# The end of the first MoE in a retention + MoE + MoE kernel: a weight slice split earlier, a rounding on another engine, two blocks and the logits in another order

## The chip, the cores and the metric

The kernel runs on one core of a Trainium2 chip. The core has TensorE (matmuls, results in PSUM banks), VectorE, ScalarE and GpSimd (elementwise work), and SyncE, which issues DMAs. Each engine runs its own queue in order and waits on semaphores for the others. The metric is the device time of one execution in microseconds.

## The reference

Three layers in a row: a retention (attention with a decaying state), a dense feed-forward layer with the mish activation ("the first MoE"), and a mixture of eight experts in which each token goes to the one expert with the largest logit.

```python
x = attn_out.transpose(0, 2, 1, 3).reshape(B * S, H * D)     # 1536 tokens x 512

h = x @ w_in                                                 # 512 x 2048
sp = np.where(h > 20.0, h, np.log1p(np.exp(np.minimum(h, 20.0))))
x = (h * np.tanh(sp)) @ w_out                                # mish, 2048 x 512

logits = x @ w_gate                                          # 8 experts
e_idx = np.argmax(logits, axis=1)
gate_w = softmax(logits)[np.arange(N), e_idx]
eom = 1.0 / (1.0 + np.exp(-(x @ w_output_gate)))
for e in range(E):
    mask = e_idx == e
    h = np.maximum(x[mask] @ w1[e], 0.0)
    out[mask] = gate_w[mask, None] * eom[mask, e, None] * (h @ w2[e])
```

## The kernel before

**Numbers.** Every large product is made of three fast matmuls: each operand is split into a rounded part and a remainder (`hi`, `lo`), and hi·hi, hi·lo and lo·hi are added in PSUM. So a weight slice or an activation must be *rounded* (a cast, `copy`, L311) and then have its *remainder* taken (a subtraction on VectorE) before TensorE can use it. For weights this is `split` (L221): `split_in` for `w_in`, with the rounding on ScalarE, and `split_out` for `w_out`, with both steps on VectorE (`split(..., V, V)`). The split slices of `w_out` live in a ring of six tiles, that is three slices.

**The first MoE.** The 1536 tokens are worked on in two groups of six blocks of 128 tokens. Per group there are 16 slices of 128 hidden units; slice `i` runs from 0 to 31 over both groups. For a slice, `up` multiplies (into `hps`), `take_h` copies the result and takes a sigmoid on ScalarE, `mish_ln` and `mish_tanh` make mish from it: a logarithm and a tanh on ScalarE, each with a table load ahead of it where the table changes, and then a product on VectorE (L263). `mish_split` rounds this product (L267, on the engine given to it) and takes its remainder on VectorE (L268). `down` adds the slice's contribution to the six accumulators `acc[0]` to `acc[5]`, one per block of tokens: three matmuls (L278, L279, L280) for each block. L278 and L279 need the rounded activation, L280 its remainder.

Logarithm and tanh run for two slices at a time, save for the last two, 30 and 31 (`NS - 2`, `NS - 1`), which run one by one. `down` is three slices behind `up`, so after the loop over slices `down` of 29, 30 and 31 remain.

**The stage after the loop** (L725 to L788) joins the first MoE with the routing of the last six blocks. Block by block (`tb`) it ends the accumulation of slices 30 and 31, takes the finished rows out (`take_rows`, and `part_rows` with a rounding on ScalarE, L496, and a subtraction on GpSimd, L497), turns the rows of the block before (`turn_rows`, four TensorE transposes, L318, and a copy), and for pairs of blocks makes the logits (`logits_of`, L339), turns them (`turn_logits`, L349 and the copy L350), picks the expert (`pick`, `weigh`, L363 to L384, small VectorE operations), ranks the tokens (`rank`, two matmuls, L393 and L394), finds their places (`place`, L402 to L406), builds a selection matrix (`select`, L485) and sends the rows to their places in DRAM (`send`, VectorE and indirect DMAs from GpSimd's queue, L421). Instead of reading the rows of expert 0 back from DRAM, TensorE adds them: `turn_base` (L472) starts the banks with what was already there, and `add_rows` (L504) multiplies the selection with the rows. When the last pair is in, `split_x` makes the input of expert 0, and the second MoE begins.

**What sets the order.** TensorE, VectorE and ScalarE run in the order in which the code issues (`manual_schedule`); there is no planner for them. GpSimd's and SyncE's queues are ordered by the scheduler of the framework.

Of the kernel before, what the change touches and what calls it, by code (L numbers as in the profile page):

```python
# [65 lines left out]
def retention_moe_moe(ctx: ExitStack, tc: tile.TileContext, qkv, wraw, w12, wg, cst, pad, out):  # L66
    nc = tc.nc
    V, A, T, G, SP = nc.vector, nc.scalar, nc.tensor, nc.gpsimd, nc.sync
# [15 lines left out]
    def he(w, dtype=F32):  # L84

        return h_p.tile([P, GT], dtype, name="h")[:, 0:w]

    acc, hps = [], []
# [141 lines left out]
    NS = NG * NF  # L230
# [26 lines left out]
    def mish_ln(b):  # L257
        for i in b:
            A.activation(out=es[i], in_=es[i], func=AF.Ln, bias=tiny)

    def mish_tanh(i):
        A.activation(out=es[i], in_=es[i], func=AF.Tanh, scale=-1.0)  # L262
        V.tensor_tensor(out=hs[i], in0=hs[i], in1=es.pop(i), op=ALU.mult)  # L263

    def mish_split(i, engine):
        h, gh, gl = hs.pop(i), he(GT, F32R), he(GT, F32R)
        copy(engine, gh, h)  # L267
        V.tensor_tensor(out=gl, in0=h, in1=gh.bitcast(F32), op=ALU.subtract)  # L268
        gs[i] = gh, gl

    def down(i, tbs):
        g, f = divmod(i, NF)
        wh, wl = wout[i]
        gh, gl = gs[i]
        for tb in tbs:
            o = acc[tb]
            c = slice(tb * P, (tb + 1) * P)
            T.matmul(out=o, lhsT=gh[:, c], rhs=wh, start=(f == 0), stop=False)  # L278
            T.matmul(out=o, lhsT=gh[:, c], rhs=wl, start=False, stop=False)  # L279
            T.matmul(out=o, lhsT=gl[:, c], rhs=wh, start=False, stop=(f == NF - 1))  # L280
        if tbs[-1] == GB - 1:
            del wout[i], gs[i]
# [28 lines left out]
    def copy(engine, to, of):  # L311
        (A.copy if engine is A else engine.tensor_copy)(out=to, in_=of)  # L312

    def turn_rows(b, o, engine):
        r = rows[b // 2][:, b % 2]
        x = he(KD * P)
        for k in range(KD):
            T.transpose(out=o[:, k * P:(k + 1) * P], in_=r[:, k * P:(k + 1) * P], identity=ident)  # L318
        copy(engine, x, o)
        xts[b] = [x[:, k * P:(k + 1) * P] for k in range(KD)]  # L320
# [13 lines left out]
    def logits_of(b0, n, o):  # L334

        w, v = 32 * n, int(b0 < NB - GB)
        for k in range(KD):
            for b in range(n):
                T.matmul(out=o[b * 32:(b + 1) * 32, 0:P], lhsT=wgs[:, v, k], rhs=xts[b0 + b][k],  # L339
                         start=(k == 0), stop=(k == KD - 1))  # L340
        x = [xts.pop(b0 + b) for b in range(n)][0]
        lt, l = spare.pop(b0) if v else x[0:2]
        lt, l = lt[0:w], l[:, 0:w]
        A.copy(out=lt, in_=o[0:w, 0:P])
        return lt, l
# [9 lines left out]
    def tl(name, n, w, dtype=F32):  # L355
        return r_p.tile([P, n, w], dtype, name=f"{name}{n}", bufs=3 if n == 2 else 1)
# [19 lines left out]
    def weigh(b0, n, o):  # L376

        lz = o.rearrange("p (b e) -> p b e", b=n)
        l, z = lz[:, :, 0:E], lz[:, :, E:2 * E]
        m, ohb = chosen[b0]["m"], chosen[b0]["ohb"]  # L380
        d, t = tl("d", n, E + 1), tl("t", n, E)
        V.tensor_tensor(out=d[:, :, 0:E], in0=l, in1=m.to_broadcast([P, n, E]), op=ALU.subtract)
        V.tensor_tensor(out=t, in0=z, in1=ohb, op=ALU.mult)
        V.tensor_reduce(out=d[:, :, E:E + 1], in_=t, axis=AX.X, op=ALU.add, negate=True)  # L384
        chosen[b0]["d"] = d

    def exps(b0):
        d = chosen[b0]["d"]
        A.activation(out=d, in_=d, func=AF.Exp)
# [77 lines left out]
    def turn_base(banks):  # L467

        r = xrow[0]
        for k in banks:  # L470
            for b in range(2):
                T.matmul(out=xbank[k][:, b * CB2:(b + 1) * CB2], lhsT=r[0:CB2, b, k * P:(k + 1) * P],  # L472
                         rhs=ident[0:CB2, 0:CB2],
                         start=(not begun[k]), stop=False)
                begun[k] = True
# [24 lines left out]
    def add_rows(b0, n, banks, last=False):  # L500
        for k in banks:
            for b in range(b0, b0 + n):
                for i, x in enumerate(parts[b]):
                    T.matmul(out=xbank[k][:, 0:CAP], lhsT=x[:, k * P:(k + 1) * P], rhs=sel[b], start=(not begun[k]),  # L504
                             stop=(last and b == b0 + n - 1 and i == 1))
                    begun[k] = True
# [89 lines left out]
    def split_in(i):  # L596
        if i < NS:
            win[i] = split(fw[i % NF][:, 0], "wi")

    def split_out(i):  # L600
        if 0 <= i < NS:
            wout[i] = split(fw[i % NF][:, 1], "wo", V, V)
# [27 lines left out]
    with tc.manual_schedule(engines={A.engine, T.engine, V.engine}):  # L630
# [36 lines left out]
        for i in range(NS):  # L667
            b, c = batch_at.get(i - 1, []), batch_at.get(i - 2, [])
            j = i - NF - LAG
            s0 = ND + 4 * min(i, 3) + 34 * max(0, i - 3) // 5 + 2  # L670
            mish_ln(b)
            steps_to(s0)
            late = range(NA + 2 * i, min(NA + 2 * i + 2, NU))
            if late:
                sm = scores(late[0], acc[0:2])
            up(i, 0)
            if late:
                values(late[0], acc[0:2], sm)
                sm = scores(late[1], acc[2:4])
                for n in late:  # L680
                    if n + 2 < NU:
                        prep_unit(n + 2)
            split_out(i + 2 - LAG)
            take_h(i, 0)
            if len(c) == 2:
                mish_split(c[1], A)
            if b:
                mish_tanh(b[0])
            split_in(i + 2)
            steps_to(s0 + 2)  # L690
            up(i, 1)
            if late:
                values(late[1], acc[2:4], sm)
            take_h(i, 1)
            if len(b) == 2:
                mish_tanh(b[1])
            if b:
                mish_split(b[0], A)

            if j == 1:  # L700
                turn_pair(0)
                turn_pair(2)
            if j == 3:
                turn_pair(4)
            steps_to(s0 + 4)
            if i >= LAG:
                down(i - LAG, range(0, 3))
                route(j)
                down(i - LAG, range(3, GB))
            if j == -1:  # L710
                for tb in range(GB):
                    take_rows(tb, A if tb % 2 else V)
                    if tb % 2:
                        keep(tb - 1)
            if j == 0:
                r = x_p.tile([P, KD * GT], F32, name="xl")
                for tb in range(0, GB, 2):
                    xpair[tb] = load_blocks(xall[tb * P:(tb + 2) * P], r[:, 512 * tb:512 * tb + 1024])
            if j == 10:
                load_rows(0)  # L720
            if 6 <= i < 6 + E:
                A.dma_start(out=xs[(i - 6) * CAP:(i - 5) * CAP], in_=pad)
            if j >= 0:
                load_w12(j)
        g = NG - 1  # L725
        b0 = g * GB
        mish_ln([NS - 1])
        mish_tanh(NS - 1)
        mish_split(NS - 1, A)
        split_out(NS - 1)  # L730
        down(NS - 3, range(GB))
        for m in range(NF - LAG, NF):
            load_w12(m)
        splits2(0, True, True)
# [2 lines left out]
        la, ra, rc, lb, rb = (acc[0][:, 0:4 * E], acc[1][:, 0:2 * E], acc[1][:, 2 * E:4 * E], hps[1][:, 0:4 * E],  # L737
                              acc[1][:, 4 * E:6 * E])
        for tb in range(GB):
            down(NS - 2, [tb])  # L740
            if tb:
                turn_rows(b0 + tb - 1, hps[tb % 2], V if tb < 3 else A)
            if tb in (3, 5):
                n = b0 + tb - 3
                lg[0] = turn_logits(acc[0], *lg[0])
                pick(n, 2, lg[0])
                weigh(n, 2, lg[0])
            if tb == 4:
                turn_base([0, 1])
                add_rows(b0, 2, [0])  # L750
            if tb == 5:
                turn_base([2])
            down(NS - 1, [tb])
            if tb in (3, 5):
                o = ra if tb == 3 else rc
                rank(n, 2, o)
                place(n, 2, o)
                select(n, 0)
                select(n, 1)
            if tb == 4:  # L760
                add_rows(b0, 2, [1])
            take_rows(b0 + tb, A)
            part_rows(b0 + tb, acc[tb])
            if tb in (3, 5):
                exps(n)
                send(n, 2)
            if tb in (2, 4):
                lg[0] = logits_of(b0 + tb - 2, 2, acc[0])
        add_rows(b0, 2, [2])
        turn_rows(b0 + 5, hps[0], A)  # L770
        logits(b0 + 4, lb[:, 0:2 * E])
# [169 lines left out]
```

## Time and profile before

| what | value |
|---|---|
| median of 3 runs | 563.82 us (563.41 to 564.87) |
| the profiled execution | 561.92 us |
| its span, first to last instruction | 560.2 us |
| TensorE matmul busy | 539.9 us (96% of the span) |
| VectorE busy | 369.2 us (66%) |
| ScalarE busy | 378.6 us (68%) |
| GpSimd busy | 75.7 us (14%) |
| mean granted TensorE clock | 0.993 |

All rows below are of the one profiled execution. A timeline lists, for one engine, when an instruction started, how long it took, its line, what it wrote and read with the shape, how often in a row it ran, and in brackets how long the engine had been idle before it and who released it. Matmuls are pipelined, so a matmul of 0.39 us can follow its predecessor after 0.23 us. The granted clock is a share of full speed: 1.00 is 2.4 GHz. Idle time of an engine counts only where the chain of waits runs through it.

### The profile page before, as it was taken

To read this page: it belongs to the slowest core of one execution; us is meant where nothing else is said; L and a number is where in the kernel's file an instruction comes from. 1 tells how busy PE (TensorE), PEld (TensorE's weight loads), DVE (VectorE), ACT (ScalarE), POOL (GpSimd) and SP (SyncE) were. 2 spreads that over 40 slices of the span, in tenths; PEclk is the share of its full clock that TensorE was granted. 3 is DMA by queue.
4 is the path that set the end of the run, shared out by engine and by line. 5 is a ranking of instruction groups with operands and counts; after the bars stand their busy time and mean duration, and the time that the engine had idled before them with its cause. 6 is when DMAs were issued, how large, how long until landed. Compare 5 with 4: busy or idle time off the path is not lost.

```text
span 560.2 us, 9429 instructions
## 1 busy us (share of the span) xinstructions
PE 539.9 (96%) x3311; PEld 451.9 (81%) x3311; DVE 369.2 (66%) x790; ACT 378.6 (68%) x722; POOL 75.7 (14%) x130
## 2 busy tenths in 40 slices
PE   8999989999999999999999997989999999999992
PEld 4555578899899999989898895778888888888881
DVE  3788867888888753655356435587777677677560
ACT  5667649978887886767767777445766666666551
POOL 3445410000000100000001500530101101101001
PEclk9999999999999999999999999999999999999997
DMA  8889721245454102661221621327999866671001
GB/s 304 290 262 297 261 77 65 78 147 167 154 179 138 42 1 76 175 163 45 70 76 37 220 78 45 144 84 190 220 295 340 269 214 206 212 212 52 2 22 36
DMA packets 38116, 83.22 MB, mean 149 GB/s; under 512 B 5858, under 2 KB 15970, under 8 KB 37936
## 3 DMA queue, kind: packets, MB, share of 16 engines
q1 hardware_dynamic: 34848, 71.70, 41.8%
q0 software_dynamic: 2240, 6.31, 3.4%
q10 hardware_dynamic: 976, 4.56, 2.6%
q8 instruction: 28, 0.46, 0.3%
q14 instruction: 24, 0.20, 0.1%
HBM read 73.04 MB, written 13.72 MB: 155 GB/s over the span
## 4 chain that ended last, share of the span: by engine, by line
PE 86%; DVE 4%; issue 4%; ACT 2%; DMA 1%; POOL 0%; POOLq 0%; DVEq 0%; ACTq 0%
PE hps L244 23%; PE hps L534 13%; PE acc L278 7%; PE acc L279 7%; PE acc L280 7%; PE acc L551 5%; PE acc L550 5%; PE acc L552 5%; PE sp L148 4%; PE sp L165 2%; PE sp L169 2%; PE sp L173 1%; DMA cs<-in_cst_dram 1%; DMA h<-in_qkv_dram 1%; PE acc L148 1%
## 5 line engine op out<-in xcount | busy, mean ns | idle before, releaser
L244 PE MATMUL hps<-xh,wi 128*128 128x384 f32 x512 | 137.8, 338 | 0.0
L534 PEld LDWEIGHTS hps<-xh,wi 128*128 128x128 f32 x768 | 95.3, 191 | 7.4 <-DVE h L539 1.0
L534 PE MATMUL hps<-xh,wi 128*128 128x224 f32 x768 | 96.0, 274 | 0.8 <-DVE h L539 0.8
L244 PEld LDWEIGHTS hps<-xh,wi 128*128 128x128 f32 x512 | 93.1, 188 | 1.8 <-ACT h L255 0.3
L244 PE MATMUL hps<-xl,wi 128*128 128x384 f32 x256 | 85.7, 335 | 0.0
L225 DVE TENSOR_TENSOR wi<-fw,wi 128x512 fp32r<-128x512 f32 x96 | 66.2, 689 | 19.7 <-ACT wi L312 12.5
L278 PE MATMUL acc<-wo,h 128*128 128x512 f32 x192 | 75.9, 395 | 2.6 <-DVE wo L312 2.6
L279 PE MATMUL acc<-wo,h 128*128 128x512 f32 x192 | 75.4, 393 | 0.2 <-DVE wo L225 0.2
L280 PE MATMUL acc<-wo,h 128*128 128x512 f32 x192 | 75.5, 393 | 0.0
L225 DVE TENSOR_TENSOR wo<-fw,wo 128x512 fp32r<-128x512 f32 x96 | 66.3, 691 | 12.2 <-ACT wo L312 9.1
L263 DVE TENSOR_TENSOR h<-h 128x768 f32<-128x768 f32 x32 | 30.7, 959 | 50.6 <-ACT h L262 47.0
L254 ACT ACTIVATE h<-hps 128x384 f32<-128x384 f32 x64 | 31.4, 491 | 48.2 <-PE hps L244 48.2
L312 ACT CAST wi<-fw 128x512 fp32r<-128x512 f32 x96 | 59.0, 615 | 0.5 <-DVE fw L218 0.5
L538 ACT ACTIVATE h<-hps 128x224 fp32r<-128x224 f32 x64 | 22.8, 357 | 44.1 <-PE hps L534 43.1
L551 PE MATMUL acc<-wo,h 128*112 128x512 f32 x128 | 50.7, 396 | 0.0
L550 PE MATMUL acc<-wo,h 128*112 128x512 f32 x128 | 50.6, 395 | 0.0
L552 PE MATMUL acc<-wo,h 128*112 128x512 f32 x128 | 50.3, 393 | 0.0
L244 PEld LDWEIGHTS hps<-xl,wi 128*128 128x128 f32 x256 | 48.1, 188 | 1.2
L312 ACT CAST wo<-fw 128x512 fp32r<-128x512 f32 x64 | 39.7, 621 | 11.1 <-PE acc L551 11.0
L142 ACT ACTIVATE qz<-h,cs 128x128 f32<-128x128 f32 x96 | 33.2, 394 | 19.6 <-PE sp L148 16.6
L278 PEld LDWEIGHTS acc<-wo,h 128*128 128x128 f32 x192 | 36.1, 188 | 10.3 <-ACT wo L312 3.0
L280 PEld LDWEIGHTS acc<-wo,h 128*128 128x128 f32 x192 | 36.0, 188 | 7.9 <-DVE h L268 0.3
(140 smaller groups left out, 812.7 us busy)
## 6 DMA issues: line engine op xcount, KB each, us to landing
fw<-in_w_dram SPq DMA_DIRECT2D x64, 512.0 KB, 4.1
raw<-in_wraw_dram SPq DMA_DIRECT2D x32, 512.0 KB, 3.9
h<-in_qkv_dram SPq DMA_DIRECT2D x48, 256.0 KB, 5.2
xs<-in_pad_dram ACTq DMA_DIRECT2D x8, 449.8 KB
raw<-xs SPq DMA_DIRECT2D x28, 112.0 KB, 7.8
xall<-raw SPq DMA_DIRECT2D x6, 512.0 KB, 4.8
xl<-xall SPq DMA_DIRECT2D x12, 128.0 KB, 4.6
raw<-xs SPq DMA_DIRECT2D x2, 224.0 KB, 3.2
```

The source lines that it names most:

```text
L142: A.activation(out=qz[:, j], in_=t[:, 0], func=AF.Copy, scale=halves[:, j:j + 1])
L225: engine.tensor_tensor(out=lo, in0=src, in1=hi.bitcast(F32), op=ALU.subtract)
L244: T.matmul(out=o, lhsT=a[:, k * P:(k + 1) * P], rhs=b[:, k, c], start=(n == 0), stop=(n == 3 * KD - 1))
L254: A.activation(out=hs[i][:, c], in_=o, func=AF.Copy)
L278: T.matmul(out=o, lhsT=gh[:, c], rhs=wh, start=(f == 0), stop=False)
L279: T.matmul(out=o, lhsT=gh[:, c], rhs=wl, start=False, stop=False)
L280: T.matmul(out=o, lhsT=gl[:, c], rhs=wh, start=False, stop=(f == NF - 1))
L312: (A.copy if engine is A else engine.tensor_copy)(out=to, in_=of)
L534: T.matmul(out=o, lhsT=a[:, k * P:(k + 1) * P], rhs=x[:, k, b:b + CAP], start=(n == 0), stop=(n == 3 * KD - 1))
L550: T.matmul(out=o, lhsT=g[:, c], rhs=wh, start=(f == 0), stop=False)
L551: T.matmul(out=o, lhsT=g[:, c], rhs=wl, start=False, stop=False)
L552: T.matmul(out=o, lhsT=g[:, l], rhs=wh, start=False, stop=(f == NF2 - 1))
```

## The change

Four edits, all around the end of the loop over slices:

- In the loop's last iteration, the rounding of slice 30 (`mish_split(b[0], ...)`) goes from ScalarE to VectorE.
- `split_out(31)` is issued ahead of `mish_tanh(31)` and `mish_split(31)`, not behind them.
- `down` of slice 30 runs for blocks 0 and 1 before the loop over blocks. In the loop it runs from block 2 on, and the transposes of block 0's rows come behind slice 31's matmuls of block 1.
- For blocks 3 and 5 the logits are turned, picked and weighed ahead of the transposes of the rows, not behind them. `turn_base([2])` goes from block 5 of the loop to behind the loop.

```diff
--- before.py
+++ after.py
@@ -695,7 +695,7 @@
             if len(b) == 2:
                 mish_tanh(b[1])
             if b:
-                mish_split(b[0], A)
+                mish_split(b[0], A if i < NS - 1 else V)
 
             if j == 1:
                 turn_pair(0)
@@ -725,10 +725,11 @@
         g = NG - 1
         b0 = g * GB
         mish_ln([NS - 1])
+        split_out(NS - 1)
         mish_tanh(NS - 1)
         mish_split(NS - 1, A)
-        split_out(NS - 1)
         down(NS - 3, range(GB))
+        down(NS - 2, [0, 1])
         for m in range(NF - LAG, NF):
             load_w12(m)
         splits2(0, True, True)
@@ -737,20 +738,21 @@
         la, ra, rc, lb, rb = (acc[0][:, 0:4 * E], acc[1][:, 0:2 * E], acc[1][:, 2 * E:4 * E], hps[1][:, 0:4 * E],
                               acc[1][:, 4 * E:6 * E])
         for tb in range(GB):
-            down(NS - 2, [tb])
-            if tb:
-                turn_rows(b0 + tb - 1, hps[tb % 2], V if tb < 3 else A)
+            if tb > 1:
+                down(NS - 2, [tb])
             if tb in (3, 5):
                 n = b0 + tb - 3
                 lg[0] = turn_logits(acc[0], *lg[0])
                 pick(n, 2, lg[0])
                 weigh(n, 2, lg[0])
+            if tb > 1:
+                turn_rows(b0 + tb - 1, hps[tb % 2], V if tb < 3 else A)
             if tb == 4:
                 turn_base([0, 1])
                 add_rows(b0, 2, [0])
-            if tb == 5:
-                turn_base([2])
             down(NS - 1, [tb])
+            if tb == 1:
+                turn_rows(b0, hps[1], V)
             if tb in (3, 5):
                 o = ra if tb == 3 else rc
                 rank(n, 2, o)
@@ -766,6 +768,7 @@
                 send(n, 2)
             if tb in (2, 4):
                 lg[0] = logits_of(b0 + tb - 2, 2, acc[0])
+        turn_base([2])
         add_rows(b0, 2, [2])
         turn_rows(b0 + 5, hps[0], A)
         logits(b0 + 4, lb[:, 0:2 * E])
```

On VectorE, at the end of the loop over slices (L263 is the mish product, L268 the remainder, `L312 CAST h` a rounding of an activation, `L312 CAST wo` and `L225` rounding and remainder of an output slice):

```order
 L263 TENSOR_TENSOR h<-h 128x768
-L268 TENSOR_TENSOR h<-h 128x768
-L263 TENSOR_TENSOR h<-h 128x768
-L268 TENSOR_TENSOR h<-h 128x768
-L312 CAST wo<-fw 128x512
-L225 TENSOR_TENSOR wo<-fw,wo 128x512
+L312 CAST h<-h 128x768
+L268 TENSOR_TENSOR h<-h 128x768
+L312 CAST wo<-fw 128x512
+L225 TENSOR_TENSOR wo<-fw,wo 128x512
+L263 TENSOR_TENSOR h<-h 128x768
+L268 TENSOR_TENSOR h<-h 128x768
```

The rounding of slice 30 is new on this engine, and the two steps of the last output slice now stand ahead of the product of slice 31.

On TensorE, behind the first blocks of `down` (acc_1076 and acc_1077 are the accumulators of blocks 0 and 1):

```order
+L278 MATMUL acc_1077<-wo,h 128x512
+L279 MATMUL acc_1077<-wo,h 128x512
+L280 MATMUL acc_1077<-wo,h 128x512
 L278 MATMUL acc_1076<-wo,h 128x512
 L279 MATMUL acc_1076<-wo,h 128x512
```

Three matmuls of slice 30, for block 1, now stand ahead of the first matmul of slice 31 (the last two rows).

On TensorE, at block 5 of the stage after the loop (L349 turns the logits, L318 the rows, L472 is `turn_base`, L393 and L394 rank):

```order
+L349 MATMUL acc_1076<-cs,h 128x64
 L318 MATMUL hps_1075<-cs,raw 128x128 x4
-L349 MATMUL acc_1076<-cs,h 128x64
-L472 MATMUL acc_1080<-cs,raw 128x112 x2
 L278 MATMUL acc_1081<-wo,h 128x512
 L279 MATMUL acc_1081<-wo,h 128x512
 L280 MATMUL acc_1081<-wo,h 128x512
```

The logits are turned before the rows, and `turn_base` has left its place ahead of slice 31's matmuls; it stands behind L394 in the new order. At block 3 the two turns change places in the same way.

## Rows read from the trace of the kernel before

**Rows 1.** The page, part 4: chain that ended last, shares by engine.

```profile
PE 86%; DVE 4%; issue 4%; ACT 2%; DMA 1%; POOL 0%; POOLq 0%; DVEq 0%; ACTq 0%
```

**Rows 2.** Table by stretches: engine busy us (instructions), granted clock, DMA share, GB/s.

```profile
400.00:450.00 50.00, 50.00 (x334) 43.83 (x333) 36.04 (x65) 32.07 (x66) 6.49 (x6) 1.00 1.01 293
343.00:348.00 5.00, 2.17 (x9) 1.08 (x7) 4.00 (x7) 3.06 (x6) 0.00 (x0) 1.00 0.09 15
550.00:561.00 11.00, 0.08 (x1) 0.00 (x0) 0.00 (x0) 0.69 (x1) 1.56 (x2) 0.62 0.15 45
```

**Rows 3.** Timeline, ScalarE: start, us, line, operation, out<-in, [idle before <-releaser].

```profile
336.35 0.49 ACT L255 ACTIVATE h<-hps 128x384 f32<-128x384 f32 x1
337.23 0.84 ACT L312 CAST h<-h 128x768 fp32r<-128x768 f32 x1 [0.39 <-DVE h L263]
338.09 1.28 ACT L259 ACT_TABLE_LOAD   x1
...
343.51 0.83 ACT L312 CAST h<-h 128x768 fp32r<-128x768 f32 x1 [1.03 <-DVE h L263]
```

**Rows 4.** Timeline, VectorE, the last product and the last split.

```profile
342.52 0.96 DVE L263 TENSOR_TENSOR h<-h 128x768 f32<-128x768 f32 x1 [3.46 <-ACT h L262]
344.37 0.96 DVE L268 TENSOR_TENSOR h<-h 128x768 fp32r<-128x768 f32 x1 [0.90 <-ACT h L312]
345.25 0.42 DVE L312 CAST wo<-fw 128x512 fp32r<-128x512 f32 x1
345.77 0.69 DVE L225 TENSOR_TENSOR wo<-fw,wo 128x512 fp32r<-128x512 f32 x1
```

**Rows 5.** Timeline, TensorE, before and after its longest wait.

```profile
338.11 0.39 PE L280 MATMUL acc<-wo,h 128*128 128x512 f32 x1
...
342.87 0.39 PE L280 MATMUL acc<-wo,h 128*128 128x512 f32 x1
345.81 0.47 PE L278 MATMUL acc<-wo,h 128*128 128x512 f32 x1 [2.56 <-DVE wo L312]
...
346.85 0.40 PE L280 MATMUL acc<-wo,h 128*128 128x512 f32 x1
```

**Rows 6.** Timeline, TensorE, turns, selected rows, the last rank.

```profile
353.23 0.60 PE L318 MATMUL hps<-cs,raw 128*128 128x128 f32 x4
353.76 0.27 PE L349 MATMUL acc<-cs,h 64*128 64x64 f32 x1
...
358.27 0.73 PE L504 MATMUL acc<-h,xl 128*128 128x224 f32 x4 [0.44 <-DVE h L485]
...
369.88 0.17 PE L393 MATMUL acc<-ohb,trib 128*128 128x16 bf16 x1 [0.45 <-DVE ohb L371]
```

**Rows 7.** Timeline, VectorE, first placing and second pick.

```profile
356.27 1.16 DVE L404 TENSOR_TENSOR at<-at,far 128x16 f32<-128x16 f32 x1
357.47 0.17 DVE L405 TENSOR_TENSOR at<-at,ohb 128x16 f32<-128x16 f32 x1
...
357.88 0.58 DVE L485 TENSOR_SCALAR h<-cs,place 128x224 fp32r<-128x224 f32 x2
...
363.18 0.77 DVE L366 SCALAR_TENSOR_TENSOR c<-h,m,cs 128x8 f32<-128x8 f32 x2
```

**Rows 8.** Timeline, GpSimd, two subtractions.

```profile
356.13 1.27 POOL L497 TENSOR_TENSOR xl<-raw,xl 128x512 fp32r<-128x512 f32 x1 [2.25 <-ACT xl L496]
...
362.48 1.30 POOL L497 TENSOR_TENSOR xl<-raw,xl 128x512 fp32r<-128x512 f32 x1
```

**Rows 9.** Timelines of GpSimd and VectorE at 50 us.

```profile
50.08 0.61 POOL L138 TENSOR_TENSOR qh<-h,cs 128x128 f32<-128x128 f32 x1 [0.39 <-PE sp L169]
...
50.01 0.42 DVE L210 TENSOR_SCALAR fw<-raw 128x512 f32<-128x512 f32 x1
```

**Rows 10.** By line: L138, L485; ns min/median/max, first and last start.

```profile
L138 POOL TENSOR_TENSOR qh<-h,cs x40: 408/413/613, 9.4 to 83.5; 128x128 f32<-128x128 f32 x40
...
L485 DVE TENSOR_SCALAR h<-cs,place x6: 319/334/427, 357.9 to 371.6; 128x224 fp32r<-128x224 f32 x6
```

## The prediction

> **What bounds the kernel now.** I read the chain of waits first: it runs 86% through TensorE [rows 1], so only a change of what TensorE waits for, or of work on it, can move the end. The table by stretches says where TensorE is not fed: it is busy 50.00 of 50 us in a stretch of the second MoE, but 2.17 of 5 us from 343 to 348 us [rows 2]. No TensorE work is added or removed here, so the gain is what is taken out of such gaps, and the second MoE then shifts as a whole. I then read the timelines of TensorE, ScalarE, VectorE and GpSimd from 334 to 378 us.
>
> The gap: TensorE ends block 0 of slice 30 (342.87, one matmul each 0.227 us: from 338.11 to 342.87 there are 21) and could go on at 343.10. Its next matmul starts at 345.81, held by the rounding of the last output slice, and the third of that block only at 346.85 [rows 5]. Behind it stand two chains. ScalarE: sigmoid of slice 31 done at 336.35 + 0.49 = 336.84; then the rounding of slice 30 (0.84, which itself waited 0.39 for VectorE); then a table load at 338.09, Ln, another load, tanh, and the rounding of slice 31 at 343.51 [rows 3]. VectorE: product at 342.52, remainder at 344.37, and only then the split of the output slice, 0.42 + 0.69 from 345.25 [rows 4].
>
> After the gap TensorE and VectorE alternate: logits turned (353.76), VectorE picks and ranks, TensorE adds the selected rows (358.27) [rows 6], and all of it once more. There GpSimd matters: its subtraction L497 at 356.13 lasts 1.27 and ends at 357.40 [rows 8]; VectorE's L404, 16 columns wide, starts at 356.27 and ends at 357.43 [rows 7]. It was held by GpSimd. The next subtraction, 362.48 to 363.78, holds L366 in the same way (363.18 to 363.95).
>
> **The change part by part.**
> (a) *Rounding of slice 30 on VectorE.* ScalarE's table load no longer waits for it: 336.84 instead of 338.09, 1.25 us sooner, and Ln, tanh, product, rounding and remainder of slice 31 with it. Rounded slice 31: 343.51 + 0.83 - 1.25 = 343.09. Remainder: 344.37 + 0.96 - 1.25 = 344.08. VectorE pays for a rounding of 768 columns, which the trace of before lacks on this engine: its rounding of 512 takes 0.42 [rows 4], so between 0.42 and 1.5 x 0.42 = 0.63; I take 0.63. The product of slice 30 is done at 337.21 (ScalarE's rounding at 337.23 waited for it), so the rounding ends at 337.84 and the remainder (0.96) at 338.80. TensorE wants it at about 342.4. Cost nothing.
> (b) *Output slice split ahead of the product.* In VectorE's order the 0.42 + 0.69 now stand before the product of slice 31, at 338.80 to 339.91, and the product starts at 342.52 - 1.25 = 341.27: 1.36 us of slack. What would be queued behind a wait here is that product, hence everything. The split needs the buffers of slice 28; the last matmul that reads them starts at 338.11 and ends at 338.50 [rows 5]: in time by 0.30. The weight load of the SyncE queue behind this split is issued sooner; it is for a late slice of the second MoE and costs nothing.
> (c) *Block 1 of slice 30 first.* Three matmuls, 0.68 us, now run from 343.10 to 343.78, in the old gap. The rounded slice 31 (343.09) and both halves of the weights are there by then, so slice 31 starts at 343.78. Its third matmul needs the remainder (344.08) and a weight load, so about 344.3 instead of 346.85: **2.55**. Block 1 of slice 30 is behind it as well: **0.68**.
> (d) *Logits turned ahead of the row transposes.* The four transposes before the turn at 353.76 start at 353.23, and so 0.53 lie ahead of VectorE's chain; they go behind the turn, into the time in which TensorE waits for VectorE. **0.53** the first time. Up to the first turn: 2.55 + 0.68 + 0.53 = 3.76, so it starts at 350.00.
> (e) *What is late next.* The moved transposes delay the block that feeds the GpSimd subtraction by the same 0.53 against the turn. Before, the subtraction started 356.13 - 353.76 = 2.37 behind the turn; now 2.90, ending at 4.17. VectorE's L404 comes 356.27 - 353.76 = 2.51 behind the turn and now gets through, and L405 behind it. The select L485 comes 0.62 behind a free L404 (357.88 - 357.43 = 0.45 from its end, and 0.17 for 16 columns as L405 at 357.47 [rows 7]). It would start at 3.13, inside the subtraction. Does GpSimd hold it? The 512-column TENSOR_SCALAR at 50.01 takes 0.42, and the GpSimd product begun under it at 50.08 takes 0.61 instead of the median 0.413 [rows 9, 10]: that instruction and GpSimd exclude each other. The select is of the same kind and, it seems, of the same pace: between 0.17 for 16 columns and 0.69 for 512 (345.77 [rows 4]) a plain operation of 224 would take 0.39, between 0.17 and 0.42 a quick one 0.28; the select's median is 0.334 and its least 0.319, with a scalar to fetch [rows 10]. So it starts at 4.17 behind the turn; before, at 357.88 - 353.76 = 4.12. The first turn thus wins no more than its 0.53; bounds: 1.0 gained if the select is not held, 0.4 lost if L405 too is caught. I take the hold, by [rows 9, 10].
> The Trainium skill ("SBUF — State Buffer", section "Who interferes with whom") says that such a tensor_scalar can take the port pair that VectorE and GpSimd share, that a two-input operation in SBUF contends with GpSimd's reads, and that whichever is second waits in full. The trace agrees (held to 357.43, subtraction to 357.40); by the page the sum stays at 3.8, without it 4.75.
> (f) *Second turn.* GpSimd's next subtraction follows the select at a fixed distance (362.48 - 357.88 = 4.60: weights written, then two indirect transfers from the same queue). It therefore comes 3.76 sooner. The second turn comes another 0.53 sooner, but the L366 behind it falls into that subtraction as before. The 0.53 becomes waiting on TensorE: gain **0**, up to 0.4 if L366 slips through. The last subtraction falls into the same chain before and after; I give it 0.2 either way.
> (g) *turn_base([2])* leaves the wait before the rank product and goes behind it, ahead of the last logits: four short matmuls, about 0.4 us. The third pick has TensorE waiting 0.45 for VectorE (369.88) [rows 6], which covers it. With the cover gone, 0.4.
> Sum: 3.76, rounded to **3.8 us**. The profiled execution (561.92 us, span 560.2) would become 558.1 and 556.4; against the median of the runs, 563.82 - 3.8 = **560.0**. The profiled execution lies 1.9 below that median and the three runs spread over 1.5, so I allow 0.5 for this.
>
> **Rivals.**
> *The select is not held.* Then VectorE's chain gains 1.0 more, and the subtraction that follows it too: 3.76 + 1.0 = 4.75, so 559.1. For it: the select uses a scalar from memory, which the 50.01 row does not. Against it: its pace, which is not that of a plain operation.
> *Another hold.* All three GpSimd subtractions lie within 0.2 us of a VectorE operation that they can stop. If one more is caught in full it costs 1.3: gain 2.5, 561.3. For it: the margins. Against it: holds of 1.2 and about 0.6 stand in [rows 7] already, and a hold moves the later work with it.
> *The split waits in VectorE's queue.* If the buffers came free only when slice 29 is done (342.4) instead of 28, the split would end at 343.5, the product would start 2.2 late, and slice 31's third matmul would come at 346.5: the gain falls to 0.3 + 0.68 + 0.53 = 1.5, 562.3. Against it: the split takes the buffers six tiles back, three slices.
> *Slower: the TensorE clock.* The granted clock is 1.00 from 343 to 348, through the longest gap, and 0.62 in the last stretch, where TensorE is idle [rows 2]. The change breaks one gap into shorter waits. If the chip answered with the lower level (1.2 GHz) in the alternating stage, its TensorE time would double: a loss begins at 3.8 us of added time. Such work fills most of the stage, and 9 us of it would take 9 more, less some 1 us of waits that it fills (0.44 and 0.45 in [rows 6]): 563.8 - 3.8 + 8 = 568. Against it: the longer gap of before did not do it.
>
> **How the numbers follow.** Forecast 0.62 (560.0; its own range 559.3 to 561.0 with run noise). Select not held 0.12, another hold 0.16, the split waiting 0.06, the clock 0.04. About 0.3%, 1.7 us, is what can be told from no change. Faster: the first three, 0.90; same: 0.06; slower: 0.04. The range reaches from the free select less 0.5 of noise, 558.6, to the extra hold plus 0.5, 561.8.
>
> **What would show it.** In the new trace: the table load for Ln right after the sigmoid at 336.8; the weights' split on VectorE near 339; TensorE's wait near 343 gone, slice 31 starting at 343.8; the first turn near 350.0; the select starting where the GpSimd subtraction ends; the third rank at 366.1 instead of 369.88, and the second MoE as long as before. I am wrong if TensorE still waits over 0.5 us before slice 31, or if what is won at the first turn is not there at the last pick.

## The result and the profile after

| | before | changed |
|---|---|---|
| median of 4 runs | 563.83 us (563.41 to 564.87) | 558.47 us (557.34 to 559.80) |
| ratio | | 0.9903 (95% interval 0.9877 to 0.9929) |
| the profiled execution, and its span | 561.92, 560.2 us | 558.71, 556.8 us |
| TensorE matmul busy | 539.9 us | 539.2 us |

The change is faster by 5.4 us (4.0 to 6.9 by the interval). 560.0 was forecast, and the median lies 0.1 us below the lower end of the forecast range, 558.6. The profiled executions alone differ by 3.2 us, so the first question is what the medians contain that these two traces do not show.

First the steps, in the trace of the changed kernel. ScalarE (columns as in [rows 3]): the table load now follows the sigmoid at once, and the rounding of slice 31 starts at 342.45, not 343.51.

```profile
336.52 0.49 ACT L255 ACTIVATE h<-hps 128x384 f32<-128x384 f32 x1
337.03 1.28 ACT L259 ACT_TABLE_LOAD   x1
...
342.45 0.83 ACT L312 CAST h<-h 128x768 fp32r<-128x768 f32 x1 [1.02 <-DVE h L263]
```

VectorE: the rounding of slice 30 takes 0.56 us here, the output slice is split from 338.88 on, and then comes the last product. It was 1.37 us idle ahead of it, so nothing was held up.

```profile
337.40 0.56 DVE L312 CAST h<-h 128x768 fp32r<-128x768 f32 x1
...
338.88 0.42 DVE L312 CAST wo<-fw 128x512 fp32r<-128x512 f32 x1
...
341.46 0.96 DVE L263 TENSOR_TENSOR h<-h 128x768 f32<-128x768 f32 x1 [1.37 <-ACT h L262]
343.32 0.96 DVE L268 TENSOR_TENSOR h<-h 128x768 fp32r<-128x768 f32 x1 [0.90 <-ACT h L312]
```

The table by stretches (columns as in [rows 2]) shows TensorE busy for 4.97 of the 5 us from 343 to 348, where it was 2.17:

```profile
343.00:348.00 5.00, 4.97 (x26) 3.48 (x26) 4.08 (x6) 3.92 (x8) 1.92 (x2) 1.00 0.30 95
```

TensorE, against [rows 5, 6]: slice 31 starts at 343.94 without a wait, its third matmul is at 344.40, the first turn of the logits at 350.01, the selected rows at 354.23, the last two ranks at 360.37 and 365.93.

```profile
343.94 0.39 PE L278 MATMUL acc<-wo,h 128*128 128x512 f32 x1
344.17 0.39 PE L279 MATMUL acc<-wo,h 128*128 128x512 f32 x1
344.40 0.43 PE L280 MATMUL acc<-wo,h 128*128 128x512 f32 x1
...
350.01 0.27 PE L349 MATMUL acc<-cs,h 64*128 64x64 f32 x1
...
354.23 0.73 PE L504 MATMUL acc<-h,xl 128*128 128x224 f32 x4
...
360.37 0.17 PE L393 MATMUL acc<-ohb,trib 128*128 128x16 bf16 x1 [0.90 <-DVE ohb L371]
...
365.93 0.17 PE L393 MATMUL acc<-ohb,trib 128*128 128x16 bf16 x1
```

For comparing executions I use the *stage*: on TensorE, from the start of the last matmul of the last `up` (the last L244, below "the last up matmul") to the start of the first matmul of the second MoE (the first L534 behind it). The numbers below are starts on TensorE less that of the last up matmul, so that the 0.2 us by which executions differ before it drop out.

| landmark, us behind the last up matmul | before | changed | gained |
|---|---|---|---|
| slice 31, block 0, third matmul (L280) | 12.81 | 10.19 | 2.62 |
| first turn of the logits (L349) | 19.72 | 15.80 | 3.92 |
| selected rows of the first pair (L504) | 24.23 | 20.02 | 4.21 |
| second turn (L349) | 28.36 | 23.70 | 4.66 |
| second rank (L393) | 30.37 | 26.16 | 4.21 |
| third rank (L393) | 35.84 | 31.72 | 4.12 |
| first matmul of the second MoE (L534): the stage | 39.57 | 35.45 | 4.12 |

### The profile page after: what moved, and what is told of

It reads as the page before. It is cut to its first block, busy times and chain, and to the rows that moved or that the text cites. A ratio compares the mean times of both kernels' runs of the same rounds, so it can differ in the third digit from the quotient of the medians.

```text
span 556.8 us, 9428 instructions
## 1 busy us (share of the span) xinstructions
PE 539.2 (97%) x3311; PEld 451.7 (81%) x3311; DVE 369.9 (66%) x791; ACT 377.2 (68%) x721; POOL 76.0 (14%) x130
## 3 DMA queue, kind: packets, MB, share of 16 engines
q10 hardware_dynamic: 976, 4.56, 2.6%
## 4 chain that ended last, share of the span: by engine, by line
PE 90%; issue 4%; DVE 3%; ACT 1%; POOL 0%; POOLq 0%
PE hps L244 24%; PE hps L534 13%; PE acc L278 8%; PE acc L280 8%; PE acc L279 8%; PE acc L551 5%; PE acc L550 5%; PE acc L552 5%; PE sp L148 5%; PE sp L165 2%; PE sp L169 2%; PE sp L173 1%; PE acc L504 1%; PE idle L648 1%; PE acc L148 1%
## 5 line engine op out<-in xcount | busy, mean ns | idle before, releaser
L244 PE MATMUL hps<-xh,wi 128*128 128x384 f32 x512 | 137.7, 338 | 0.0
L534 PEld LDWEIGHTS hps<-xh,wi 128*128 128x128 f32 x768 | 95.3, 191 | 7.4 <-DVE h L539 1.0
L534 PE MATMUL hps<-xh,wi 128*128 128x224 f32 x768 | 96.0, 274 | 0.8 <-DVE h L539 0.8
L244 PEld LDWEIGHTS hps<-xh,wi 128*128 128x128 f32 x512 | 93.1, 188 | 1.8 <-ACT h L255 0.4
L244 PE MATMUL hps<-xl,wi 128*128 128x384 f32 x256 | 85.7, 335 | 0.0
L225 DVE TENSOR_TENSOR wi<-fw,wi 128x512 fp32r<-128x512 f32 x96 | 66.2, 689 | 19.6 <-ACT wi L312 16.2
L280 PE MATMUL acc<-wo,h 128*128 128x512 f32 x192 | 75.5, 393 | 0.0
L225 DVE TENSOR_TENSOR wo<-fw,wo 128x512 fp32r<-128x512 f32 x96 | 66.3, 690 | 12.1 <-ACT wo L312 9.0
L263 DVE TENSOR_TENSOR h<-h 128x768 f32<-128x768 f32 x32 | 30.7, 959 | 48.5 <-ACT h L262 48.5
L312 ACT CAST wi<-fw 128x512 fp32r<-128x512 f32 x96 | 59.0, 615 | 0.5 <-DVE fw L218 0.5
L244 PEld LDWEIGHTS hps<-xl,wi 128*128 128x128 f32 x256 | 48.1, 188 | 1.2
L312 ACT CAST wo<-fw 128x512 fp32r<-128x512 f32 x64 | 39.6, 619 | 11.2 <-PE acc L551 11.0
L280 PEld LDWEIGHTS acc<-wo,h 128*128 128x128 f32 x192 | 36.0, 188 | 8.1 <-DVE h L268 0.5
```

What stands on the lines that cost most here:

```text
L225: engine.tensor_tensor(out=lo, in0=src, in1=hi.bitcast(F32), op=ALU.subtract)
L244: T.matmul(out=o, lhsT=a[:, k * P:(k + 1) * P], rhs=b[:, k, c], start=(n == 0), stop=(n == 3 * KD - 1))
L534: T.matmul(out=o, lhsT=a[:, k * P:(k + 1) * P], rhs=x[:, k, b:b + CAP], start=(n == 0), stop=(n == 3 * KD - 1))
```

## The experiments

Theory A: the change is worth the 4.1 us of the stage, and the rest is scatter. Theory B: it also shortens something outside the stage. Theory C came out of the first of these runs: the lower TensorE clock.

**The kernel before, once more.**

> The kernel before once more, unchanged. 'Stage' is the time on TensorE from the start of the last matmul of the last up product (L244) to the start of the first matmul of the second MoE (L534); before it is 39.57 us, in the changed kernel 35.45 us. Theory A (the change is worth what the stage shows, 4.1 us; the rest of the measured 5.4 us is scatter outside the stage, between executions): ratio 1.000 within 0.002, stage 39.5 to 39.7, and the time less the stage scatters by 1 to 2 us between executions of one and the same kernel. Theory B (the change also shortens something outside the stage by 1.3 us): ratio 1.000 too, but the time less the stage is near 524.2 us in every execution, against 523.0 for the changed kernel.

Ratio 1.0005 (0.9991 to 1.0019) over 12 runs, from 562.25 to 565.20 us, so the same time. But the profiled execution had a stage of 40.80 us, not 39.57. The same stretches in the first trace of before, and in this one:

```profile
342.00:346.00 4.00, 1.44 (x7) 0.90 (x5) 2.48 (x4) 2.87 (x5) 0.00 (x0) 1.00 0.00 0
346.00:350.00 4.00, 3.73 (x16) 2.30 (x16) 2.96 (x5) 1.73 (x4) 1.29 (x1) 1.00 0.52 153
```

```profile
342.00:346.00 4.00, 1.44 (x7) 0.85 (x5) 2.54 (x4) 2.82 (x5) 0.00 (x0) 1.00 0.00 0
346.00:350.00 4.00, 3.77 (x12) 2.87 (x12) 2.37 (x5) 1.08 (x2) 1.07 (x1) 0.57 0.59 161
```

The granted clock is 0.57 of full speed from 346 to 350 us: for part of it TensorE ran at 1.2 GHz and not at 2.4. In front of it stands the long wait of [rows 5]; behind it matmuls of 128x512 take 0.63 us and not 0.39:

```profile
345.76 0.47 PE L278 MATMUL acc<-wo,h 128*128 128x512 f32 x1 [2.56 <-DVE wo L312]
346.46 0.80 PE L279 MATMUL acc<-wo,h 128*128 128x512 f32 x1 [0.23 <-DVE wo L225]
347.06 0.63 PE L280 MATMUL acc<-wo,h 128*128 128x512 f32 x1
```

So the kernel before has a second price here, 40.80 - 39.57 = 1.23 us, and its first trace happened to be an execution that did not pay it. This is theory C: the wait is followed, in most executions, by some us at the lower clock. The next runs test it.

**The changed kernel, once more.**

> The changed kernel once more, unchanged. Stage 35.4 to 35.6 us by both theories. Theory A: 4.1 us faster, ratio 0.9927 (0.991 to 0.994). Theory B: 5.4 us faster, ratio 0.9905 or less.

557.91 us, ratio 0.9895 (0.9873 to 0.9916): 5.9 us faster by the ratio, 5.4 us by the medians (before, run beside it: 563.29). The stage is 35.46 us, with a clock of 1.00 throughout. Theory A's 0.9927 lies outside the interval. Time less stage is 558.30 - 35.46 = 522.84 here and 523.26 in the first trace of the changed kernel; it is 522.35 and 523.11 in the two of before. Theory B falls: outside the stage nothing got shorter.

**Two more traces of before.**

> The kernel before, unchanged, for a third trace. Theory C: time is stage plus 522.3 to 523.3 us in every execution, and a stage above 39.6 has a stretch at the lower clock in it, in about three of four executions (from the timed runs: 42 of 52 lie above 562.8 us). Theory A: stage 39.6 at a clock of 1.00 throughout, and the time scatters outside the stage.

> The kernel before, unchanged, for a fourth trace; as for the third. If the drop sits behind the long wait, the granted clock is under 1.00 between 344 and 351 us; if late in the stage, between 362 and 374 us.

Stages 40.81 and 40.80, times 564.32 and 564.80. Both have the drop right behind the wait. Everything lies 1.2 us later in these two. The third trace (first fence) and the fourth (second fence):

```profile
342.00:346.00 4.00, 2.42 (x11) 1.68 (x9) 1.43 (x2) 2.96 (x5) 0.00 (x0) 1.00 0.00 0
346.00:350.00 4.00, 2.80 (x11) 1.92 (x11) 3.31 (x6) 2.14 (x5) 0.34 (x1) 0.86 0.33 106
350.00:354.00 4.00, 4.00 (x20) 2.98 (x20) 1.38 (x2) 1.25 (x3) 2.20 (x2) 0.72 0.70 252
```

```profile
346.00:350.00 4.00, 2.85 (x10) 2.06 (x11) 3.27 (x6) 2.10 (x4) 0.39 (x1) 0.80 0.35 108
350.00:354.00 4.00, 4.00 (x21) 2.93 (x21) 1.38 (x2) 1.33 (x3) 2.04 (x2) 0.78 0.67 237
```

In three of four traces of before the wait is followed by the lower clock, for the same 1.23 us each time. Both executions also had a drop near 72 us, at the end of the first layer, which is why they run late: the last up matmul starts at 335.20 and 335.16, not at 333.9 to 334.4 as in the traces without that drop, so it cost 1.1 to 1.2 us. With this taken off, time less stage is 522.3 and 522.9. Over all 14 traces of this study, so corrected, it lies between 522.2 and 523.3.

The mean granted clock of every timed run says the same for the executions that were not traced. The trace of before without a drop has a mean of 0.993, those with one or two have 0.990 to 0.988. Of 52 further runs of before, 9 have 0.993 or more; their mean time is 562.0 us. The other 43 average 563.6, and all 52 average 563.3. Of the eight runs of the changed kernel, six have 0.993 or more; they average 557.9. The other two are its second trace (0.992, without a drop) and the slowest run (0.987, 559.80); all eight average 558.15. The mean parts the runs only roughly, since it also contains the lower clock at the end of every execution [rows 2]. But between the runs of 0.993 or more the two kernels differ by 562.0 - 557.9 = 4.1 us, which is the gain of the stage, and between all of them by 5.2 us.

**The wait filled.** In the kernel before, TensorE runs ten matmuls whose result nobody reads while it waits; nothing else is changed.

```diff
             down(NS - 2, [tb])
+            if tb == 0:
+                for _ in range(10):
+                    T.matmul(out=hps[0], lhsT=gs[NS - 2][0][:, 0:P], rhs=wout[NS - 2][0], start=True, stop=True)
```

> The kernel before with ten idle-work matmuls (128x512, into a bank that nobody reads) on TensorE in its long wait before slice 31; all else is unchanged. Ten at 0.227 us are 2.3 us, from 343.1 to 345.4, and the wait ends at 345.8, so they delay nothing: stage 39.57 us when the granted clock stays at 1.00. Theory C (in most executions of the kernel before the wait is followed by some us at the lower clock, as in the second trace of before: 0.57 from 346 to 350 us, stage 40.80): no drop behind the gap, time 1.0 to 1.5 us below before, ratio 0.9975. Theory A (scatter outside the stage): ratio 1.000, between 0.9985 and 1.0015.

```profile
343.38 2.43 PE L743 MATMUL hps<-wo,h 128*128 128x512 f32 x10
346.10 0.47 PE L278 MATMUL acc<-wo,h 128*128 128x512 f32 x1 [0.29 <-DVE wo L312]
```

The filling delays nothing: the third matmul of slice 31 comes 12.80 us behind the last up matmul. The clock (stretches from 342, 346 and 366 us):

```profile
342.00:346.00 4.00, 3.81 (x17) 2.81 (x15) 2.25 (x3) 2.98 (x5) 0.00 (x0) 1.00 0.00 0
346.00:350.00 4.00, 3.63 (x16) 2.49 (x16) 3.19 (x5) 1.64 (x4) 1.23 (x1) 1.00 0.51 177
366.00:370.00 4.00, 4.00 (x27) 4.00 (x26) 3.66 (x21) 0.59 (x1) 1.23 (x2) 0.69 0.30 116
```

No drop behind the gap; instead one late in the stage, around the last pick; stage 40.30. The median is 562.53, ratio 0.9991 (0.9981 to 1.0002): 0.5 us faster by the ratio and 0.7 by the medians, not the 1.0 to 1.5 that theory C expected. The 0.9975 of theory C is outside the interval, so the saving is smaller than it expected, and the interval contains the 1.000 of theory A. The single runs say more. Without any drop in the stage or near 72 us an execution takes 39.57 + 522.2 to 523.3 = 561.8 to 562.9. Of the 52 runs of before 42 lie above 562.8, of the 12 filled runs four do; a mean clock of 0.993 or more have 5 of the 23 runs of before beside them, and 6 of the 12. In the one trace, with work in the gap there is no drop behind it, and there is one at another place; that the filling moved it there is not shown.

**The wait put back into the changed kernel.**

```diff
         split_out(NS - 1)
+        for _ in range(4):
+            A.activation(out=es[NS - 1], in_=es[NS - 1], func=AF.Copy)
         mish_tanh(NS - 1)
```

> The changed kernel with a wait put back: four copies of 768 columns in place, about 0.85 us each, on ScalarE ahead of the last tanh. They delay slice 31 by 3.4 to 3.5 us, and TensorE waits about 2.8 us before it. Without any change of the clock the stage would be 35.45 + 3.45 = 38.9 us and the time 558.2 + 3.45 = 561.6, ratio 0.9968 (theory A). Theory C: in most executions the wait is followed by a drop of the clock that costs 1.2 us more: 562.8, ratio 0.999, and the stage is 40.1 in such an execution.

563.45 us, ratio 1.0008 (0.9997 to 1.0019). Slice 31 came 3.46 us later (13.65 against 10.19), so without the clock 561.4 to 561.9 would follow from the two medians of the changed kernel; measured is 1.5 to 2.1 more. That is also more than the 562.8 of theory C. The trace shows why: it has the drop behind the wait and a longer one late in the stage, and a stage of 41.99 instead of 38.9:

```profile
346.00:350.00 4.00, 3.34 (x9) 2.31 (x10) 2.76 (x4) 3.48 (x7) 0.30 (x1) 0.58 0.06 18
366.00:370.00 4.00, 3.97 (x25) 3.88 (x24) 3.59 (x25) 0.69 (x2) 0.66 (x2) 0.64 0.15 57
370.00:374.00 4.00, 4.00 (x22) 3.93 (x22) 1.52 (x10) 0.00 (x0) 1.47 (x2) 0.51 0.34 132
```

Theory A's ratio of 0.9968 is outside the interval. All 12 runs have a mean clock of 0.990 or less, against one of the eight runs of the changed kernel without the wait. A wait of TensorE at this place costs its length and, in most executions, a clock drop on top.

**The edits one by one.**

> The kernel before with the first edit alone, slice 30 rounded on VectorE. ScalarE's chain starts 1.25 us sooner, and the last output slice is still split behind the last remainder: first matmul of slice 31 (block 0) and everything behind it 1.25 us sooner, 11.56 us behind the last up matmul for the third matmul of block 0, not 12.81. Stage 38.3 us at full clock. Theory C: the wait is still 1.3 us, a drop of the clock can follow it or come late in the stage, 1.2 us more each time.

> The kernel before with the second edit alone, the last output slice split ahead of the last product. Slice 31 then waits for the rounded slice (344.35) and its remainder (345.33) alone; third matmul of block 0 about 345.6 instead of 346.85, 1.3 us sooner (11.5 us behind the last up matmul). Stage 38.3 us at full clock. With the run before: the two edits add up to the 2.6 us that they give together. Rival: either alone gives under 0.5, because the other chain stays late.

> The kernel before with the first two edits alone: slice 30 rounded on VectorE, and the last output slice split ahead of the last product. Theory: the third matmul of slice 31 for block 0 comes 2.5 us sooner; TensorE has no more work for the rest of the gap and waits some 0.7 us for the remainder. Stage 39.57 - 2.55 = 37.0 us. Rival: block 1 of slice 30 is not what fills the gap, and these two edits give 3.2 us, stage 36.3.

| edits | third matmul of slice 31, block 0 | gained there | stage |
|---|---|---|---|
| none | 12.81 | | 39.57 |
| rounding of slice 30 on VectorE | 11.59 | 1.22 | 38.36 |
| output slice split first | 11.33 | 1.48 | 38.22 |
| both | 10.12 | 2.69 | 38.68, with a drop |

Each of the two gives its own part, and 1.22 + 1.48 = 2.70 is what both give (2.69); the rival of under 0.5 for either alone falls. The two waited in a row, not side by side: first the rounded slice, then the split behind its remainder. The stages of the single edits hold no drop. The stage of both together came to 38.68 and not to the 37.0 expected: the clock fell late in the stage, and near 72 us as well:

```profile
70.00:74.00 4.00, 2.67 (x16) 2.26 (x16) 3.34 (x10) 1.45 (x5) 0.84 (x3) 0.78 0.27 93
366.00:370.00 4.00, 4.00 (x20) 3.93 (x21) 2.61 (x21) 0.00 (x0) 1.85 (x2) 0.50 0.17 66
370.00:374.00 4.00, 4.00 (x26) 3.98 (x25) 1.83 (x11) 0.85 (x4) 0.12 (x1) 0.67 0.19 72
```

At the second rank, ahead of the late drop, both edits together are 2.59 us ahead of before (27.78 against 30.37), near the 2.55 expected; the rival of 3.2 falls.

**The turn of the logits undone.**

> The changed kernel with its fourth edit undone: rows are transposed ahead of the turn of the logits again, and turn_base([2]) is back in block 5. Theory of the prediction, with the size that the trace after shows (a hold by GpSimd lasts only about 1.1 us, not the recorded 1.27): the edit is worth 0.53 at the first turn and 0.29 at the select, nothing at the second turn; stage 35.45 + 0.82 = 36.3 us. Rival 1, the prediction as written (hold of 1.27): 0.5, stage 35.95. Rival 2, the hold takes all of it back: stage 35.5.

```profile
350.15 0.27 PE L349 MATMUL acc<-cs,h 64*128 64x64 f32 x1
...
354.67 0.73 PE L504 MATMUL acc<-h,xl 128*128 128x224 f32 x4 [0.43 <-DVE h L485]
...
360.81 0.17 PE L393 MATMUL acc<-ohb,trib 128*128 128x16 bf16 x1 [0.42 <-DVE ohb L371]
```

Behind the last up matmul (333.90) the first turn comes at 16.25, against 15.80 in the changed kernel, the selected rows at 20.77 against 20.02, the second rank at 26.91 against 26.16. So the fourth edit gives 0.45 us at the turn, where 0.53 was expected, and 0.30 more at the select, where VectorE gets past L404 before it is held. The 0.75 lies between the 0.5 of rival 1 and the 0.82 of the first theory, nearer to the theory; rival 2, that the hold takes it all back, falls. The stage was 36.62, with a drop in the last pick (0.77 and 0.80), so the end of the stage does not tell the two sizes apart:

```profile
362.00:366.00 4.00, 4.00 (x30) 4.00 (x29) 3.68 (x20) 0.59 (x1) 1.23 (x2) 0.77 0.35 130
366.00:370.00 4.00, 3.85 (x28) 3.60 (x28) 2.20 (x13) 0.22 (x1) 1.60 (x2) 0.80 0.34 132
```

This version, set against the one with two edits, also gives the size of the third edit, at the second rank, ahead of the drops at the end of the stage: two edits are 2.59 us ahead of before, three are 3.46, all four 4.21. The third edit, block 1 of slice 30 in the gap and the transposes of block 0 behind it, is thus worth 0.87 us.

**The holds by GpSimd.** In the changed kernel VectorE's select (353.15), L366 of the second pick and L383 are held, by these three GpSimd subtractions:

```profile
352.52 0.17 DVE L404 TENSOR_TENSOR at<-at,far 128x16 f32<-128x16 f32 x1
352.73 0.18 DVE L405 TENSOR_TENSOR at<-at,ohb 128x16 f32<-128x16 f32 x1
...
353.15 1.27 DVE L485 TENSOR_SCALAR h<-cs,place 128x224 fp32r<-128x224 f32 x2
...
358.69 1.22 DVE L366 SCALAR_TENSOR_TENSOR c<-h,m,cs 128x8 f32<-128x8 f32 x2
...
360.72 1.27 DVE L383 TENSOR_TENSOR t<-h,ohb 128x16 f32<-128x16 f32 x1
```

```profile
352.77 1.28 POOL L497 TENSOR_TENSOR xl<-raw,xl 128x512 fp32r<-128x512 f32 x1 [2.20 <-ACT xl L496]
...
358.44 1.30 POOL L497 TENSOR_TENSOR xl<-raw,xl 128x512 fp32r<-128x512 f32 x1
360.67 1.29 POOL L497 TENSOR_TENSOR xl<-raw,xl 128x512 fp32r<-128x512 f32 x1 [0.93 <-ACT xl L496]
```

The two selects together take 1.27 us where they took 0.58 [rows 7]. Two versions move subtractions from GpSimd to VectorE (the edit shown moves all three; the other has `n == 3` and moves that of block 3 alone):

```diff
-        G.tensor_tensor(out=lo, in0=r, in1=hi.bitcast(F32), op=ALU.subtract)
+        (V if n >= 3 else G).tensor_tensor(out=lo, in0=r, in1=hi.bitcast(F32), op=ALU.subtract)
```

> The changed kernel with the subtraction of block 3 alone on VectorE. Theory of the holds: the two selects take 0.58 us and not 1.27, TensorE starts the selected rows (L504) 4.0 us behind the turn and not 4.22, limited by its own work; behind the select stands the moved subtraction, 0.69 us, so the weights, the two indirect transfers and the next GpSimd subtraction come no more than 0.3 us sooner. That subtraction holds the second pick as before. Stage 35.1 to 35.5 us. Rival (the select is slow for a reason of its own): L485 x2 takes 1.27 us again and L504 starts 4.2 us behind the turn.

> The changed kernel with the last three subtractions of part_rows (blocks 3, 4 and 5) on VectorE and not on GpSimd, so that none of them can hold VectorE. Each costs VectorE about 0.69 us. Theory of the holds: the first select starts 1.0 us sooner behind the turn (at 3.1), L366 of the second pick takes 0.36 instead of 1.22, L383 0.17 instead of 1.27. TensorE becomes the limit in places (it is ready for the selected rows 0.3 to 0.4 us before the select today, and waits 0.9 and 0.05 us at the next two ranks), and the third subtraction of 0.69 stands ahead of the third pick: stage 34.3 to 35.0 us, 0.5 to 1.1 below the changed kernel. Rival: VectorE's own time takes the place of the holds, stage 35.4 to 35.8.

With block 3 alone (first fence) the select is free, and L504 starts 19.66 - 15.81 = 3.85 us behind the turn, where 4.0 was expected. The next hold still stands and is longer, 1.53; the stage is 35.23 us. With all three (second fence) none of the three holds is left:

```profile
352.95 0.58 DVE L485 TENSOR_SCALAR h<-cs,place 128x224 fp32r<-128x224 f32 x2
...
358.08 1.53 DVE L366 SCALAR_TENSOR_TENSOR c<-h,m,cs 128x8 f32<-128x8 f32 x2
```

```profile
352.96 0.58 DVE L485 TENSOR_SCALAR h<-cs,place 128x224 fp32r<-128x224 f32 x2
353.46 0.68 DVE L497 TENSOR_TENSOR xl<-raw,xl 128x512 fp32r<-128x512 f32 x1
...
358.09 0.36 DVE L366 SCALAR_TENSOR_TENSOR c<-h,m,cs 128x8 f32<-128x8 f32 x2
...
359.27 0.17 DVE L383 TENSOR_TENSOR t<-h,ohb 128x16 f32<-128x16 f32 x1
```

The rival, a select that is slow by itself, falls. The stage is 33.66 us, 1.8 below the changed kernel and 0.6 below the lower end of what I had expected. In the trace the moved subtraction of block 4 (356.26) lies in VectorE's idle time, and VectorE waits again after that of block 3, before the second turn, so neither delays that turn. Timed: 556.37 us (555.91 to 557.37), ratio to before 0.9889 (0.9871 to 0.9907). This version has the lowest median of the study. Its interval overlaps that of the changed kernel (0.9895), so that it is faster rests on the stage, of which there is one trace.

## Why the prediction was wrong

The direction was right, and the parts of the change worked as described; the size was 3.8 us where 5.4 was measured, and 5.4 by the medians or 5.9 by the ratio the second time. One cost of the kernel before is missing from the sum, and some terms are mis-sized. Point by point:

- **(a), (b), (c)**: as forecast. The third matmul of slice 31 came 2.62 us sooner (forecast 2.55), block 1 of slice 30 ran in the gap, and the split did not wait in VectorE's queue, so *the split waits* did not come. The rounding of 768 columns took 0.56, between the bounds. The first two edits alone gave 1.22 and 1.48, near the 1.25 of (a) and the 2.55 - 1.25 = 1.30 that it leaves for (b). The third edit, forecast at 0.68 for block 1, is worth 0.87; where the other 0.19 comes from was not traced.
- **(d)**: the first turn was forecast at 350.00 and measured at 350.01. That it agrees so well is in part luck: the execution ran 0.17 late before the gap. The gain was 3.92 us instead of 3.76, and of it the turn alone gave 0.45, not 0.53.
- **(e)**: the hold of the select came as forecast, so *the select is not held* did not come, but **the length of the hold was mis-sized**. I ended it with the recorded end of the GpSimd operation, 1.27 us. The two selects end at 353.15 + 1.27 = 354.42 and take 0.58 when free, so the first began to run at 353.84: 1.07 us behind the recorded start of the subtraction. In [rows 7, 8] the same could have been read: L404 ends at 357.43 and takes 0.17 when free, so it ran from 357.26, 1.13 us behind 356.13. The selected rows (L504) start 0.39 behind the select before (358.27 - 357.88), so 4.17 + 0.39 = 4.56 behind the turn was forecast for them; they came at 4.22, 0.34 us sooner, and the gain was 4.21 there. The Trainium skill ("Perfetto Trace Analysis", section "GPSIMD Engine Instruction") warns that the recorded span of a GpSimd instruction is not a reliable duration; the trace agrees: the holds ended 0.14 and 0.21 us ahead of the recorded ends.
- **(f)**: as forecast. The second turn gained 4.66, and the hold of L366, 1.22 instead of 0.77, took it back to 4.21. The last subtraction held L404 before (365.33, 1.19 us) and holds L383 in the changed kernel (1.27); the third rank lost 0.09 by it at most. So there are three holds before and three after, and *another hold* did not come.
- **(g)**: cost 0, as forecast.
- **The step that failed is the clock,** which the sum puts at nothing for the kernel before. I took the granted clock of before from one trace, 1.00 from 343 to 348 us, and wrote against the fourth rival that "the longer gap of before did not do it". In three of four traces it does, for 1.23 us. The prediction has the lower clock only as a rival that makes the changed kernel slower; it was a cost of the kernel before, and the change takes it away together with the wait. The stage alone, 4.12 us, would have put the median at 559.7, inside the range. There was a sign: the profiled execution lay 1.9 us below the median of the runs, and I put that down to noise of 0.5.

The sum with the clock: 4.12 + 3/4 x 1.23 = 5.0 us. It is inside both intervals (4.0 to 6.9, and 4.7 to 7.2 by the second ratio), and near the 5.2 us by which the 52 and the eight runs differ on average; between the runs with a mean clock of 0.993 or more they differ by 4.1, and the other 1.1 goes with the lower clock. Which drops make it up is not settled. Executions with a drop near 72 us occur (3 of 14 traces, none of them of the changed kernel), and drops late in the stage occur in four traces of altered kernels, in none of the four that have the new order of turn and transposes without an added wait; that these few traces tell a difference of the kernels is argued, not shown. The Trainium skill ("TensorE: Matmul & The Clock Gate", section "Why this matters for your kernels") advises to keep idle gaps between bursts of matmuls short because the clock falls behind them; the traces agree on this, with 1.23 us in three of four executions of the kernel before.

## What to carry to other kernels

A long wait of TensorE can cost more than its length: look at the granted clock behind it in several executions, and if the profiled execution is faster than the median of the runs, ask what the others pay that it does not. Where two waits stand in a row on one path, either edit gives its part; order the work so that what is ready fills the gap. A GpSimd subtraction beside a VectorE chain held it at L404, L366, L383 and the select; moving three of them to VectorE, where each takes some 0.69 us and not 1.28, shortened the stage by 1.8 us.

## What was not expected of the hardware

The lower clock comes in some executions of one and the same program and not in others: three of four traces of before, each time for 1.23 us at the same place. It also comes late in the stage, where no wait of over 1 us stands ahead of it (0.50 and 0.67 in the trace with two edits). And the hold by GpSimd is shorter than the recorded GpSimd instruction: the select, which is held as the two-input operations are (0.58 became 1.27 us, and 0.58 again when GpSimd did not run beside it), began to run 1.07 us behind the start of a subtraction recorded as 1.28.
